# Strided-sparse attention and an ELU MLP on one core: load order, transposes, P v tiles and fillers of the first batches rearranged, and a half-step schedule for later scores and P v

## The chip, the core and the metric

The kernel runs on one core of one Trainium2 chip. The metric is the device time of one execution in microseconds (us). One core has five engines that matter here: TensorE (PE; matmuls, and PEld for its weight loads), VectorE (DVE), ScalarE (ACT), GpSimd (POOL) and the DMA queues. SBUF is the on-chip memory that holds the tiles; PSUM is the memory that TensorE's results go to, and this kernel uses eight banks of it.

The profile gives a "granted clock" of TensorE: 1.00 is full speed, 0.50 is half. "Fast" and "slow" mean here only that a run lies within, or above, 1.5% of the fastest run of the same kernel on that chip.

## The reference

```python
def _attn_ref(q, k, v):                       # 8 batches, 8 heads, 576 positions, 64 columns
    scores = scale * np.matmul(q, k.transpose(0, 1, 3, 2))
    rel = pos[:, None] - pos[None, :]
    mask_local   = (rel >= 0) & (rel < 32)                          # heads 0-3
    mask_strided = (rel >= 0) & (pos[None, :] % 32 == pos[:, None] % 32)   # heads 4-7
    ...                                       # masked softmax
    return np.matmul(attn, v)

def _moe_ref(x, w_in, w_out):                 # x: 4608 tokens x 512; w_in 512x2048; w_out 2048x512
    h = x @ w_in
    g = np.where(h > 0.0, h, np.exp(np.minimum(h, 0.0)) - 1.0)
    return g @ w_out
```

The output of the attention, heads side by side, is `x` of the MLP.

## The kernel before

The attention of one batch is cut in pieces: four pairs of heads (0 and 1 local, 2 and 3 strided), each with two halves `u`. The letters in the program's schedule strings are these.

- `T`: eight or six transposes each of q and k of a head pair on TensorE, through PSUM, and two copies to SBUF.
- `S`: scores of a half, exp on ACT, the mask multiplied in on DVE. The result is `pm`.
- `M`: row sums (`ones`) and P v of a half. `E`: logarithm and exp on ACT make the reciprocal of the sums, and DVE writes `xT`, the MLP's input. `X` is `M` and `E` together. `O` is the same work by another form, used from batch 3 on; there q and k are transposed by DMA.
- `f`: "fillers", matmuls on constants that only keep TensorE's clock up.
- `2`: one L2 group, four 128x512 matmuls of `g @ w_out`.
- `A` and `B`: `M` of batch 1's local heads in two-bank and in one-bank tiles. `t`: the strided transposes of batch 2. The small letters `c`, `m`, `v`, `a`, `w`, `x` are casts, masks and loads.

The MLP works on 256 tokens at a time: eight L1 groups (eight 128x256 matmuls of `x @ w_in`) and eight L2 groups. The first 16 L1 groups stand ahead of a loop of 128. I call its turns "steps". Attention of later batches is hung into the steps as jobs.

```python
    p_pm = ctx.enter_context(tc.tile_pool(name="pms", bufs=5))
    p_x = ...(name="ps_x", bufs=2, PSUM)      # two tiles of two banks ("wide")
    p_h = ...(name="ps_h", bufs=3, PSUM)      # three tiles of one bank
    p_o = ...(name="ps_o", bufs=1, PSUM)
    # --- loads of batch 0 (cut) ---
    load_vl(0, nc.gpsimd)
    load_str(0, qs, q)
    load_str(0, ks, k)
    ...
    load_str(0, vs, v)
    for i in range(2):
        nc.gpsimd.dma_start(out=w_in_sb[:, :, i * 1024:(i + 1) * 1024],
                            in_=w_in_v[:, :, i * 1024:(i + 1) * 1024])
    # --- batch 0 (cut) ---
    spins(24)
    ...
    for it in ("S0 c T1 S1 S2 S3 f4 M0 M1 E0 m T2 M2 E1 S4 E2 M3 T3 S5 E3 "
               "S6 M4 S7 E4 M5 E5 M6 E6 M7 f8 E7").split():
        ...
    # --- batch 1 among the L2 groups of the first 512 tokens (cut) ---
    for it in ("S4 2 S5 2 X4 2 S6 2 X5 2 S7 2 X6 2 X7 2 v "
               "a 2 T0 2 S0 T1 2 S1 S2 2 S3 w 2 A0 A1 2 B2 E0 E1 E2 A3 E3 x").split():
        ...
    # --- jobs of the loop (cut) ---
    SC = {2: (3, 6, 9, 12), 3: (18, 21.5, 25, 28.5)}
    SC.update({b: tuple(33 + 18 * (b - 4) + 4.5 * i for i in range(4)) for b in range(4, B)})
    at(4, lambda: casts(2))                   # six casts on GpSimd
    for b in (2, 3): ...                      # half u at step SC+u, its P v one step later
    for b in range(4, B):
        for i, p in enumerate((2, 3, 0, 1)):
            at(SC[b][i], lambda b=b, p=p: do(("SS", b, p)))       # both halves together
            at(SC[b][i] + 1.3, lambda b=b, p=p: do(("O", b, p, 0)))
            at(SC[b][i] + 2.5, lambda b=b, p=p: do(("O", b, p, 1)))
```

The softmax here doesn't subtract the row's maximum and nothing guards it: scores larger than these inputs give would overflow.

## Time and profile before

Three runs took 354.35 to 354.86 us, with a median of 354.75. The stages below are read from the starts of matmuls in TensorE's timeline of the profiled run, whose span is 352.3 us.

| point | us |
|---|---|
| first MLP matmul | 30.37 |
| first L2 group | 47.90 |
| step 0 of the loop | 73.63 |
| step 7 | 91.77 |
| step 16 (batch 3 begins) | 113.47 |
| step 33 (batches 4 to 7 begin) | 155.91 |
| end of the last matmul | 348.17 |

These are three lines of the profile's page: TensorE's busy time, the granted clock in 40 slices of 8.8 us (tenths, 9 is whole), and the shares of the chain of waits that ended last.

```profile
PE 320.1 (91%) x2896; PEld 223.6 (63%) x2896; DVE 247.6 (70%) x479; ACT 219.6 (62%) x426; POOL 111.2 (32%) x125
...
PEclk9556998989999999999999999989999999999999
...
PE 57%; DVE 17%; DMA 11%; ACT 8%; issue 3%; POOL 2%; DVEq 0%; SPq 0%; POOLq 0%; ACTq 0%
```

TensorE is busy 91% of the span, yet it makes up only 57% of the chain: in the first 155 us the chain goes through other engines and DMA. The clock is half in the second and third slice and in most of the fourth, and drops again in the seventh, the ninth and the 27th. From the clock's records, the half-clock stretches are 8.2 to 32.1, 52.6 to 56.0, 76.5 to 79.9 and 230.1 to 233.5 us.

The next view is the windows of kernel before. The columns are the window, its length, busy us and instruction counts of PE, PEld, DVE, ACT and POOL, the granted clock, the DMA share and GB/s. The windows are the opening, batch 1, and steps 0 to 7.

```profile
10.00:30.00 20.00, 15.99 (x183) 9.89 (x181) 10.40 (x25) 11.22 (x24) 5.48 (x8) 0.50 1.17 198
47.90:73.60 25.70, 21.31 (x208) 9.58 (x204) 12.61 (x25) 14.60 (x29) 6.33 (x8) 0.93 0.72 126
73.60:91.70 18.10, 14.26 (x162) 10.73 (x162) 12.60 (x22) 10.98 (x23) 10.65 (x10) 0.91 0.49 90
```

The opening has 4 us of gaps and half clock; the two other windows have about 4 us of gaps each. The gaps are named by TensorE's timeline of kernel before. Its columns are start, busy us, what ran, and in brackets the idle time ahead of it with what ended it.

```profile
17.45 0.66 PE L228 MATMUL tp<-identity,ks 72*128 72x72 bf16 x8 [1.01 <-DMA ks<-in_k_dram]
...
27.12 0.45 PE L328 MATMUL s_ps<-pm,ones 72*64 72x288 bf16 x2 [0.32 <-ACT ln L345]
...
28.07 0.45 PE L328 MATMUL s_ps<-pm,ones 72*64 72x288 bf16 x2 [0.26 <-ACT ln L345]
...
30.37 2.76 PE L388 MATMUL hpw<-xT,w_in_sb 128*128 128x256 bf16 x16
...
75.17 0.93 PE L362 MATMUL hps<-xT,w_in_sb 128*128 128x256 bf16 x7 [1.24 <-DVE xT L277]
...
84.36 0.31 PE L328 MATMUL so<-pm,ones 72*64 72x288 bf16 x2 [2.16 <-DVE pm L258]
```

The strided keys arrive at 17.45 us. At the end of the opening a P v piece comes every 0.95 us. At steps 0 to 7 TensorE waits 1.24 us for `xT` and 2.16 us for `pm`.

The last view of kernel before is the list of TensorE's waits in batch 3 (113 to 156 us): who waited for whom, us in total, times, and the longest.

```profile
PE ox L305 <- DVE pm L264: 2.8, 4, 0.8
PE sc L253 <- DMA ksT<-ks: 1.8, 2, 1.3
PE ox L305 <- DVE pm L258: 1.7, 3, 0.7
```

Nearly every P v piece of batch 3 waits for its mask product, because it stands only one step behind its scores.

### The profile page before, as it was taken

What the parts mean: (1) busy time and instruction counts of PE and PEld (TensorE: products, weight loads), DVE (VectorE), ACT (ScalarE), POOL (GpSimd) and SP (SyncE); (2) the same over time, 40 slices, a digit from 0 to 9 for tenths busy, and PEclk for the clock granted to TensorE, in tenths of its full rate; (3) what the DMA queues carried; (4) which work ended last, traced back from release to release, by engine and by line L of the source; (5) the groups of instructions that cost most, each with busy time, mean ns of one, the idle gap of its engine ahead of it and who ended that gap; (6) DMA issues with size and microseconds to landing.
All of it is one profiled execution on the core that took longest, in us unless ns stands there. A gap on an engine that the chain in (4) does not pass through costs nothing.

```text
span 352.3 us, 7511 instructions
## 1 busy us (share of the span) xinstructions
PE 320.1 (91%) x2896; PEld 223.6 (63%) x2896; DVE 247.6 (70%) x479; ACT 219.6 (62%) x426; POOL 111.2 (32%) x125
## 2 busy tenths in 40 slices
PE   6789979777989888889999999899999999999995
PEld 4447853355666565557767766667677777677762
DVE  2552982548777678868888889848988888666660
ACT  3545755565776676758776777567768787444441
POOL 8226610367256605333445451063500000000000
PEclk9556998989999999999999999989999999999999
DMA  8999993961598998099939971599356111111111
GB/s 181 181 205 204 210 169 52 186 129 21 113 174 176 140 187 196 11 154 183 197 94 146 225 178 32 104 163 233 92 100 106 32 36 54 34 31 30 41 50 60
DMA packets 49739, 43.24 MB, mean 123 GB/s; under 512 B 32809, under 2 KB 39721, under 8 KB 49705
## 3 DMA queue, kind: packets, MB, share of 16 engines
q0 software_dynamic: 15600, 25.77, 42.7%
q1 hardware_dynamic: 32624, 16.13, 22.1%
q10 hardware_dynamic: 1480, 0.88, 1.2%
q8 instruction: 22, 0.36, 0.5%
q14 instruction: 13, 0.10, 0.1%
HBM read 38.21 MB, written 9.44 MB: 135 GB/s over the span
## 4 chain that ended last, share of the span: by engine, by line
PE 57%; DVE 17%; DMA 11%; ACT 8%; issue 3%; POOL 2%; DVEq 0%; SPq 0%; POOLq 0%; ACTq 0%
PE ops L421 25%; PE hps L362 22%; DVE g L378 4%; DMA ksT<-ks 4%; DMA vl<-in_v_dram 4%; DMA ks<-in_k_dram 4%; DVE he L377 4%; PE ox L305 3%; PE sc L253 2%; DVE xT L277 2%; DVE xT L273 2%; ACT rc L311 2%; ACT ln L309 1%; ACT ln L308 1%; DVE g L398 1%
## 5 line engine op out<-in xcount | busy, mean ns | idle before, releaser
L421 PE MATMUL ops<-w_out_sb,g 128*128 128x512 bf16 x576 | 149.1, 384 | 0.0
L362 PE MATMUL hps<-xT,w_in_sb 128*128 128x256 bf16 x1088 | 144.1, 276 | 3.2 <-DVE xT L277 2.1
L362 PEld LDWEIGHTS <-w_in_sb 128*128 128x128 bf16 x1088 | 114.6, 114 | 19.0 <-issue 3.3
L370 ACT ACTIVATE he<-hps 128x512 f32<-128x512 f32 x136 | 80.5, 594 | 50.3 <-PE hps L362 49.8
L378 DVE TENSOR_TENSOR g<-he,hps 128x512 bf16<-128x512 bf16 x130 | 89.4, 688 | 13.9 <-DVE he L377 0.5
L421 PEld LDWEIGHTS <-g 128*128 128x128 bf16 x576 | 55.7, 99 | 38.7 <-issue 1.5
L377 DVE TENSOR_SCALAR he<-he 128x512 bf16<-128x512 f32 x130 | 62.2, 478 | 17.2 <-ACT he L370 15.6
L256 ACT ACTIVATE e<-sc 128x576 bf16<-128x576 f32 (+1 forms) x64 | 39.5, 646 | 22.8 <-PE sc L253 22.8
L426 ACT COPY osb<-ops 128x512 f32<-128x512 f32 x36 | 21.1, 587 | 11.4 <-PE ops L421 11.1
L308 ACT ACTIVATE ln<-ox 64x288 f32<-64x288 f32 x40 | 16.3, 408 | 17.2 <-PE ox L305 16.9
L273 DVE TENSOR_TENSOR xT<-ox,rc 64x288 bf16<-64x288 f32 x40 | 18.2, 454 | 11.0 <-ACT rc L311 10.6
L277 DVE TENSOR_TENSOR xT<-ox,rc 64x288 bf16<-64x288 f32 x40 | 18.2, 455 | 6.9 <-ACT rc L311 6.5
L264 DVE TENSOR_TENSOR pm<-e,mask_l 128x576 bf16<-128x576 bf16 x32 | 18.3, 590 | 6.1 <-ACT e L256 5.8
L111 POOL DMA_DIRECT2D qs<-in_q_dram x8 | 6.3, 788 | 47.4 <-DMA qsT<-qs 36.0
L258 DVE TENSOR_TENSOR pm<-e,mask_s 72x576 bf16<-72x576 bf16 x32 | 14.6, 473 | 8.4 <-ACT e L256 7.9
L132 POOL COPY vsx<-vs 72x1024 bf16<-72x1024 bf16 x10 | 11.5, 1174 | 28.3 <-DMA vs<-in_v_dram 21.1
L311 ACT ACTIVATE rc<-ln 128x288 f32<-128x288 f32 x40 | 17.7, 443 | 1.3
L117 POOL CAST qlb<-ql 72x1024 bf16<-72x1024 f32 x12 | 13.4, 1117 | 9.8 <-DMA ql<-in_q_dram 9.8
L309 ACT ACTIVATE ln<-ox 64x288 f32<-64x288 f32 x40 | 16.1, 402 | 0.5
L126 POOL CAST vlx<-vl 128x768 bf16<-128x768 f32 x15 | 13.2, 906 | 8.2 <-DMA vl<-in_v_dram 8.2
L122 POOL CAST klb<-kl 96x768 bf16<-96x768 f32 x13 | 11.6, 891 | 9.9 <-DMA kl<-in_k_dram 9.9
L111 POOL DMA_DIRECT2D vs<-in_v_dram x8 | 5.7, 715 | 26.3 <-PE so L338 21.7
(87 smaller groups left out, 268.3 us busy)
## 6 DMA issues: line engine op xcount, KB each, us to landing
vl<-in_v_dram POOLq DMA_DIRECT2D x8, 576.0 KB, 16.9
out_dram<-osb SPq DMA_DIRECT2D x32, 144.0 KB
kl<-in_k_dram POOLq DMA_DIRECT2D x7, 576.0 KB, 14.1
ql<-in_q_dram POOLq DMA_DIRECT2D x7, 576.0 KB, 15.0
qs<-in_q_dram POOLq DMA_DIRECT2D x8, 288.0 KB, 6.7
ks<-in_k_dram POOLq DMA_DIRECT2D x8, 288.0 KB, 9.5
vs<-in_v_dram POOLq DMA_DIRECT2D x8, 288.0 KB, 10.7
w_in_sb<-in_moe_w_in_dram POOLq DMA_DIRECT2D x2, 1024.0 KB, 19.0
```

The costliest lines, as they stand in the source:

```text
L256: nc.scalar.activation(e[0:R], sc[0:R, :, 0:W], ACT.Exp, scale=scale)
L273: nc.vector.tensor_mul(xs[:, u * W:(u + 1) * W], o[pr], rc[pr])
L277: nc.vector.tensor_mul(dst, o[pr].rearrange(pat, b=3, s=NS), rc[pr].rearrange(pat, b=3, s=NS))
L308: nc.scalar.activation(ln[lo], o[0][hi], ACT.Ln)
L309: nc.scalar.activation(ln[hi], o[1][lo], ACT.Ln)
L311: nc.scalar.activation(rc, ln, ACT.Exp, scale=-1.0)
L362: nc.tensor.matmul(hps[:, mm], lhsT=w_in_sb[:, c, (m // 4) * 512:(m // 4 + 1) * 512].rearrange("c (p mm) -> c mm p", mm=4)[:, m % 4], rhs= ...
L370: nc.scalar.activation(e, hps, ACT.Exp)
L377: eng.tensor_scalar(e1, e, scalar1=1.0, scalar2=1.0, op0=ALU.min, op1=ALU.subtract)
L378: nc.vector.tensor_tensor(gt, e1, hps, op=ALU.max)
L421: nc.tensor.matmul(ops, lhsT=g[:, m, kk * 128:(kk + 1) * 128], rhs=w_out_sb[:, m, :], start=(m == 0), stop=(m == MC - 1))
L426: nc.scalar.copy(o_sb, ops)
```

## The change

The change wants fewer waits in the first 155 us. It has these parts.

1. Batch 0: the strided q, k and v are loaded ahead of the local v. Transposes go through tiles of one bank. All scores run first, then all P v. Fillers stand between the pieces.
2. Batch 1: P v of the local heads in one-bank tiles; two more L2 groups and the strided transposes of batch 2 (`t`) move into this stage from the loop.
3. Batch 2: its casts run at step 2 instead of 4, and batch 3's local data are loaded right behind them. Batch 3's strided q and k are loaded before the loop (`x`).
4. All of batches 2 to 7: a half-step grid. The scores of half `u` run at SC + 0.5u and their P v at SC + 1.5 + 0.5u, each half by itself. Five `pm` buffers become eight.

Smaller parts are left out here: among others, which engine casts v of batch 0, on which queue one load of q stands, and the order of the L2 groups of the second 256 tokens.

The core of the diff, with cuts marked:

```diff
-    p_pm = ctx.enter_context(tc.tile_pool(name="pms", bufs=5))
+    p_pm = ctx.enter_context(tc.tile_pool(name="pms", bufs=8))
...
-    load_vl(0, nc.gpsimd)
     load_str(0, qs, q)
     load_str(0, ks, k)
...
+    load_str(0, vs, v)
     nc.gpsimd.iota(dist, ...)
-    load_str(0, vs, v)
+    load_vl(0, nc.gpsimd)
...
+    def piece_T(b, hp, engs=None, wide=True):
+        if wide:
+            pw = p_x.tile([128, 2, 1024], BF16, tag="x", name="tp2")
+            ps = [pw[:, 0, 0:S], pw[:, 1, 0:S]]
+        else:
+            ps = [p_h.tile([128, S], BF16, tag="h", name="tp") for _ in range(2)]
...
-    for it in ("S0 c T1 S1 S2 S3 f4 M0 M1 E0 m T2 M2 E1 S4 E2 M3 T3 S5 E3 "
-               "S6 M4 S7 E4 M5 E5 M6 E6 M7 f8 E7").split():
+    for it in ("f4 S0 S1 c f4 T1 m S2 f4 T2 S3 f4 S4 T3 f4 S5 f4 S6 M4 f2 S7 f2 E4 M5 f2 E5 M6 f2 E6 "
+               "v M7 f2 E7 M0 f2 E0 M1 f2 E1 M2 f2 E2 M3 f8 E3").split():
...
-    for it in ("S4 2 S5 2 X4 2 S6 2 X5 2 S7 2 X6 2 X7 2 v "
-               "a 2 T0 2 S0 T1 2 S1 S2 2 S3 w 2 A0 A1 2 B2 E0 E1 E2 A3 E3 x").split():
+    for it in ("2 S4 2 S5 2 2 X4 2 S6 X5 2 S7 2 X6 2 X7 v "
+               "a 2 2 T0 2 S0 S1 2 T1 B0 2 S2 B1 E0 2 S3 E1 B2 2 B3 E2 2 t E3 x").split():
...
-    SC = {2: (3, 6, 9, 12), 3: (18, 21.5, 25, 28.5)}
+    SC = {2: (2, 5, 9.5, 12.5), 3: (16.5, 20.5, 24.5, 28.5)}
...
-    at(4, lambda: casts(2))
+    at(2, casts2)          # cast_k, cast_q of batch 2, load_kl/ql(3), cast_v, load_vl(3)
...
-    for b in range(4, B):
-        for i, p in enumerate((2, 3, 0, 1)):
-            at(SC[b][i], lambda b=b, p=p: do(("SS", b, p)))
-            at(SC[b][i] + 1.3, lambda b=b, p=p: do(("O", b, p, 0)))
-            at(SC[b][i] + 2.5, lambda b=b, p=p: do(("O", b, p, 1)))
+    for b in range(2, B):
+        for i, p in enumerate((2, 3, 0, 1)):
+            for u in range(2):
+                at(SC[b][i] + .5 * u, lambda b=b, p=p, u=u: do(("S", b, p, u)))
+                at(SC[b][i] + 1.5 + .5 * u,
+                   lambda b=b, p=p, u=u: do(("X" if b == 2 else "O", b, p, u)))
```

## The prediction

> **What bounds the kernel now.** TensorE: busy 320.1 of 352.3 us (engine table).  In the undisturbed stretch after 155 us, eight 128x256 matmuls and four 128x512 matmuls each take 0.86 us (timeline); 144 groups of each make 248 us, and attention of batches 1 to 7, from the same timeline (0.27 us a score piece, 0.26 to 0.42 a P v piece, 0.53 a transposed pair), about 37 us. That is 285 us. With an opening of 30.4 us (first MLP matmul in the timeline) and 4 us of last store, about 33 us are waits and half-clock time. Waits rule the first 155 us.
>
> **Where the time is (TensorE timeline, stage windows).**
> - Opening, 0 to 30.4 us. Clock 0.50 from 10 to 30 us. Strided transposes wait until 17.45 us for ks; P v then runs at 0.95 us a piece.
> - First MLP part, 30.4 to 47.7: 17.3 us for 14.8 us of work; the first 3 us run at half clock.
> - Batch 1, 47.7 to 73.4: 5.6 us of idle gaps. Clock 0.83 in two windows (50-60, 70-80): matmul groups of 0.86 take 1.7 us after the gaps.
> - Batches 2 and 3, 73.4 to 155: gaps of 2.16 (pm), 0.88, and 0.5 to 0.75 before most batch-3 P v pieces (pm), 1.34 for ksT.
>
> The Trainium skill, "TensorE: Matmul & The Clock Gate", Part 1, says that the clock is halved by an idle activity window of about 3.4 us and restored by a busy one. The trace agrees: both drops follow 1.4 to 1.6 us of gaps and last about one such window.
>
> **What the change does.**
> 1. Opening: ks and vs stand ahead of v in the queue. Estimated from about 200 GB/s: ks at 11-12 us instead of 17.4. One-bank transpose tiles let ACT copy klT without following DVE (0.45 us). All eight score pieces run first, then P v without interruption: 19 us + 8 x 0.9 + 1.7 = about 28 us to the first MLP matmul, if the 48 fillers (0.11 us each, 5 us; were 12 and 8 small ones) keep the clock. At half clock they would cost 10 us and the opening would take 32. I expect mostly full clock: -2.5 us, and -1.5 in the MLP part after it.
> 2. Batch 1: local P v in one-bank tiles, no longer competing with scores for the two wide buffers; batch 2's strided transposes cover the last xT. Gaps 5.6 to about 2.5, one or both half-clock windows gone: -4 us. Two L2 groups (1.7 us) move here from the loop.
> 3. Batch 2: transposes out of the loop, no half-clock window at 76 us, but six MLP steps without L2, where DVE (1.1 us a step plus attention) binds: -2.
> 4. Batch 3, and the half-step schedule (P v 1.5 steps after scores): most 0.5-0.75 gaps go, ksT arrives earlier: -4.
> 5. Batches 4 to 7: pm gaps of about 1.3 us go; ksT waits (1.34, 1.98 with 1.7 of half clock) stay: -0.5.
>
> Sum -14.5, partly shared, so -13.5: **341 us, range 333 to 349**. Chances: faster by over 2% 0.86, within 2% 0.12, slower 0.02.
>
> **What would show it.** First MLP matmul near 28 us; ks transposes before 13.5 us; granted clock above 0.75 in 10 to 30 us; TensorE gaps in batches 2 and 3 together under 4 us.
>
> **What would make it wrong.** Fillers at half clock delaying the chain (clock 0.5, opening 32 us); ks not earlier because the queues share bandwidth; DVE binding in the L2-free steps; more half-clock windows, or ksT waits growing in batches 4 to 7.

## The result and the profile after

Three runs took 349.60 to 350.58 us, with a median of 350.46. The ratio to kernel before is 0.9875 (95% interval 0.9848 to 0.9902). Every ratio here is the mean time of one kernel's fast runs over the mean of the other's fast runs of the same rounds, so it is not quite the ratio of the medians quoted. The gain is 1.2%: 4.3 us of the 13.5 predicted. The time lies above the upper end of the range, and the change falls under "within 2%", to which I had given 0.12.

The stages of the two profiled runs, with the changes that I predicted for them:

| stage | before | after | change | predicted |
|---|---|---|---|---|
| opening, to the first MLP matmul | 30.37 | 30.08 | -0.29 | -2.5 |
| to the first L2 group | 17.53 | 17.08 | -0.45 | -1.5 |
| batch 1, to step 0 | 25.73 | 26.09 | +0.36 | -4 |
| steps 0 to 7 | 18.14 | 18.40 | +0.26 | -2 |
| steps 7 to 16, rest of batch 2 | 21.70 | 21.89 | +0.19 | in the -2 |
| steps 16 to 33, batch 3 | 42.44 | 36.29 | -6.15 | -4 |
| step 33 to the last matmul | 192.26 | 194.96 | +2.70 | -0.5 |

Only batch 3 gained what was hoped for. The same three lines of the page, of kernel after:

```profile
PE 323.0 (93%) x2926; PEld 222.9 (64%) x2926; DVE 247.1 (71%) x479; ACT 221.0 (63%) x426; POOL 109.2 (31%) x125
...
PEclk9658999996999999999999999999999999999999
...
PE 68%; ACT 12%; DVE 11%; DMA 4%; issue 3%; SPq 1%; ACTq 0%; DVEq 0%
```

DMA has left the chain, from 11% to 4%, and TensorE's share rose. But the clock still drops in the opening, and again near 80 us, there longer than before. The half-clock stretches are now 11.8 to 28.9 and 80.1 to 86.9 us; the late one at 230 us is gone. The same windows of kernel after:

```profile
10.00:30.00 20.00, 18.44 (x194) 10.93 (x195) 9.03 (x23) 11.81 (x24) 8.73 (x10) 0.57 1.13 194
47.20:73.30 26.10, 22.75 (x255) 11.42 (x253) 13.65 (x27) 15.64 (x31) 7.31 (x9) 1.00 0.95 174
73.30:91.60 18.30, 12.40 (x136) 9.08 (x133) 12.99 (x22) 10.37 (x23) 11.15 (x13) 0.81 0.82 159
```

The opening: TensorE is busier by 2.5 us in the same 20 us, at nearly the same clock, and nothing came of it. Busy time is not progress where it is fillers. Batch 1: full clock, and more work in the same time. Steps 0 to 7: less TensorE work than before (12.40 against 14.26 us busy), in the same time, at a lower clock. TensorE's timeline of kernel after shows the places:

```profile
10.89 0.43 PE L233 MATMUL tp<-identity,klb 96*128 96x96 bf16 x6 [1.61 <-ACT klb L120]
...
13.55 0.67 PE L233 MATMUL tp<-identity,ks 72*128 72x72 bf16 x8
...
24.13 0.45 PE L333 MATMUL s_ps<-pm,ones 72*64 72x288 bf16 x2
24.37 0.45 PE L343 MATMUL o_ps<-pm,vs 72*64 72x72 bf16 x8
24.75 0.61 PE L436 MATMUL idle<-warm 128*128 128x256 bf16 x2
25.29 0.45 PE L339 MATMUL s_ps<-pm,ones 128*64 128x288 bf16 x2
...
30.08 0.27 PE L393 MATMUL hpw<-xT,w_in_sb 128*128 128x256 bf16 x1
...
74.90 1.80 PE L367 MATMUL hps<-xT,w_in_sb 128*128 128x256 bf16 x15 [1.38 <-DVE xT L282]
...
81.75 0.45 PE L333 MATMUL so<-pm,ones 72*64 72x288 bf16 x2 [3.69 <-DVE pm L263]
```

The ks transposes do come at 13.55 us, 3.9 earlier and without a wait. But a gap of 1.61 us stands ahead of them, and the clock falls at 11.8 us. At the half clock a P v piece takes 1.16 us (24.13 to 25.29) with no gap at all, and 0.54 of it (24.75 to 25.29) are two fillers at half clock. Before it took 0.95. In steps 0 to 7 the wait for `pm` grew from 2.16 to 3.69 us.

What made `pm` late is in the timeline of VectorE of kernel after (same columns):

```profile
76.98 2.23 DVE L379 SCALAR_TENSOR_TENSOR g<-he,he 128x512 bf16<-128x512 f32 x1 [2.13 <-ACT he L378]
79.13 1.04 DVE L382 TENSOR_SCALAR he<-he 128x512 bf16<-128x512 f32 x1
80.28 0.69 DVE L383 TENSOR_TENSOR g<-he,hps 128x512 bf16<-128x512 bf16 x1
80.88 1.81 DVE L263 TENSOR_TENSOR pm<-e,mask_s 72x576 bf16<-72x576 bf16 x2
```

And of GpSimd of kernel after, in the same time:

```profile
76.85 0.83 POOL L120 CAST klb<-kl 96x768 bf16<-96x768 f32 x1
77.62 1.03 POOL L117 CAST qlb<-ql 72x1024 bf16<-72x1024 f32 x1
...
80.54 1.84 POOL L126 CAST vlx<-vl 128x768 bf16<-128x768 f32 x2
```

The first instruction takes 2.23 us where it takes 0.69 elsewhere. It lies beside two casts on GpSimd. The `pm` products (1.81 for two, 0.82 undisturbed) lie beside two others. The merge at 80.28, which has one operand in PSUM, takes its usual 0.69.

The casts are not new in this stage. GpSimd works 10.65 us in it before and 11.15 after, by the windows above, and in before too VectorE is stretched beside the casts. From VectorE's timeline of kernel before:

```profile
77.25 1.51 DVE L374 SCALAR_TENSOR_TENSOR g<-he,he 128x512 bf16<-128x512 f32 x1 [2.13 <-ACT he L373]
```

And from GpSimd's timeline of kernel before:

```profile
76.41 0.83 POOL L122 CAST klb<-kl 96x768 bf16<-96x768 f32 x1
77.18 1.04 POOL L117 CAST qlb<-ql 72x1024 bf16<-72x1024 f32 x1
```

Summed over the stage, the instructions of these three kinds (the first, the second and the `pm` products) take 2.3 us more than undisturbed (0.69, 0.425 and 0.45 us) in before and 3.1 more in after.

Last, TensorE's waits in batch 3 of kernel after, in answer to the three lines of before:

```profile
PE ops L426 <- ACT osb L431: 0.9, 4, 0.2
```

The waits for `pm` and for `ksT` are gone.

### The profile page after: what moved, and what is told of

It is laid out like the page before. It is cut to its first block, busy times and chain, and to the rows that moved or that the text cites. A ratio compares the mean times of both kernels' runs of the same rounds, so it can differ in the third digit from the quotient of the medians.

```text
span 348.9 us, 7582 instructions
## 1 busy us (share of the span) xinstructions
PE 323.0 (93%) x2926; PEld 222.9 (64%) x2926; DVE 247.1 (71%) x479; ACT 221.0 (63%) x426; POOL 109.2 (31%) x125
## 4 chain that ended last, share of the span: by engine, by line
PE 68%; ACT 12%; DVE 11%; DMA 4%; issue 3%; SPq 1%; ACTq 0%; DVEq 0%
PE ops L426 28%; PE hps L367 27%; PE sc L258 4%; DVE he L382 3%; ACT he L375 3%; DVE g L383 2%; DMA kl<-in_k_dram 2%; ACT osb L431 2%; PE idle L436 2%; DMA ksT<-ks 2%; PE ox L310 1%; ACT ln L314 1%; ACT ln L313 1%; PE tp L233 1%; PE hpw L393 1%
## 5 line engine op out<-in xcount | busy, mean ns | idle before, releaser
L426 PE MATMUL ops<-w_out_sb,g 128*128 128x512 bf16 x576 | 146.9, 380 | 3.6 <-ACT osb L431 3.6
L367 PEld LDWEIGHTS <-w_in_sb 128*128 128x128 bf16 x1088 | 116.1, 114 | 22.4 <-issue 2.8
L383 DVE TENSOR_TENSOR g<-he,hps 128x512 bf16<-128x512 bf16 x130 | 89.4, 688 | 14.3 <-PE hps L367 1.0
L382 DVE TENSOR_SCALAR he<-he 128x512 bf16<-128x512 f32 x130 | 63.4, 488 | 25.2 <-ACT he L375 24.2
L426 PEld LDWEIGHTS <-g 128*128 128x128 bf16 x576 | 52.0, 98 | 44.5 <-issue 5.3
L261 ACT ACTIVATE e<-sc 128x576 bf16<-128x576 f32 (+1 forms) x64 | 41.0, 647 | 18.7 <-PE sc L258 18.6
L269 DVE TENSOR_TENSOR pm<-e,mask_l 128x576 bf16<-128x576 bf16 x32 | 15.5, 496 | 6.7 <-ACT e L261 6.5
L263 DVE TENSOR_TENSOR pm<-e,mask_s 72x576 bf16<-72x576 bf16 x32 | 15.9, 513 | 4.9 <-ACT e L261 4.9
L132 POOL COPY vsx<-vs 72x1024 bf16<-72x1024 bf16 x10 | 10.7, 1095 | 25.0 <-DMA vs<-in_v_dram 25.0
L436 PE MATMUL idle<-warm 128*128 128x256 bf16 x74 | 16.1, 367 | 1.3 <-DVE warm L155 1.3
```

The lines of the kernel that those rows point to most:

```text
L261: nc.scalar.activation(e[0:R], sc[0:R, :, 0:W], ACT.Exp, scale=scale)
L367: nc.tensor.matmul(hps[:, mm], lhsT=w_in_sb[:, c, (m // 4) * 512:(m // 4 + 1) * 512].rearrange("c (p mm) -> c mm p", mm=4)[:, m % 4], rhs= ...
L382: eng.tensor_scalar(e1, e, scalar1=1.0, scalar2=1.0, op0=ALU.min, op1=ALU.subtract)
L383: nc.vector.tensor_tensor(gt, e1, hps, op=ALU.max)
L426: nc.tensor.matmul(ops, lhsT=g[:, m, kk * 128:(kk + 1) * 128], rhs=w_out_sb[:, m, :], start=(m == 0), stop=(m == MC - 1))
L436: nc.tensor.matmul(ps, lhsT=warm[:, 0:128], rhs=warm[:, 0:ps.shape[-1]], start=True, stop=True, skip_group_check=True)
```

## The experiments

I had three questions, with a theory and a rival for each. The runs were made in four sessions on four chips. The medians of kernel before there were 354.71, 354.57, 355.06 and 355.04 us, over 7 to 11 runs each. In the third session only two of the eleven runs of kernel before count as fast, because one of them took 348.32 us; the ratios of that session are weak, and there the medians say more.

A stage scatters even where its code is the same. In eight profiled runs with the opening of kernel after, the first MLP matmul lies at 28.39 to 32.64 us and the first L2 group at 45.22 to 48.78. In the ten in which steps 0 to 7 and what stands just ahead of them are those of kernel after, these steps take 17.55 to 18.40 us. In all sixteen with batch 3 as changed, steps 16 to 33 take 36.2 to 37.8. In the twelve with the half-step grid to the end, step 33 to the last matmul takes 192.92 to 194.96, and the first trace of kernel after is the longest of these. Where I give a difference of two single traces below, read it against these ranges.

- The opening. Theory: at half clock the fillers are themselves the chain. Rival: the loads (w_in above all) bound the opening, whatever the fillers do.
- Steps 0 to 7. Theory: GpSimd's casts slow VectorE through the memory that both read. Rival: without L2 groups among these steps VectorE simply has too much work, and the casts change nothing.
- Batches 4 to 7. Theory: the half-step grid costs what the batch-3 gain brought. Rival: the difference is the draw of the clock.

### Opening: the fillers taken out (first session)

```diff
-    for it in ("f4 S0 S1 c f4 T1 m S2 f4 ... E1 M2 f2 E2 M3 f8 E3").split():
+    for it in ("S0 S1 c T1 m S2 T2 S3 S4 T3 S5 S6 M4 S7 E4 M5 E5 M6 E6 "
+               "v M7 E7 M0 E0 M1 E1 M2 E2 M3 f8 E3").split():
```

> The changed kernel without the 24 + 16 small fillers of the opening (the 26 at the start and the 8 before the MLP stay). Theory A (with the clock at half, the fillers are themselves the chain: in the changed kernel TensorE is 99% busy from 20 to 30 us and a P v piece takes 1.16 us, of which 0.54 us are two fillers): the clock stays at 0.5 all the same, but a P v piece falls back to about 0.95 us, the first MLP matmul comes at 27.5 to 28.5 us instead of 30.1, and the kernel gains 1 to 2.5 us (348 to 349.5). Theory B (the opening is bound by the order of loads and the ACT and DVE chain, fillers only fill): first MLP matmul unchanged at 30 us, time 350.5 or slower, since the clock comes back later.

Measured: 350.05 us (349.00 to 352.01, 4 runs), ratio 0.9901 (0.9837 to 0.9965). The first MLP matmul is at 27.84 instead of 30.08, ahead of all eight openings with fillers, and at half clock all the same. So the fillers were the chain at half clock, as the theory has it. But the second weight load then waits for w_in, and the clock stays half until 33.0, as TensorE's timeline of this run shows:

```profile
29.38 3.39 PE L393 MATMUL hpw<-xT,w_in_sb 128*128 128x256 bf16 x15 [1.12 <-DMA w_in_sb<-in_moe_w_in_dram]
```

These 15 matmuls take 3.39 us instead of 1.8. The first L2 group comes at 47.47, against 47.16 with fillers, and so inside the range of the eight. The rival is right about what stands behind the fillers: both bounds lie close together.

### Opening: fillers where the gap was (first session)

```diff
+            if i and mid:
+                spins(mid)              # between the two halves of one transposed pair
...
-            piece_T(0, n, None, False)
+            piece_T(0, n, None, False, 14 if n == 1 else 0)
```

> The changed kernel with 14 more fillers between the two halves of batch 0's second local transposes, where TensorE sat idle for 1.61 us just before the clock was halved. Theory A: that gap is what cost the clock; with it filled the half-clock stretch begins at 15 us or later instead of 11.8, and the first MLP matmul comes 1 to 2 us earlier (349). Theory C: the clock falls anyway at the next window, because the small pieces do not count as enough activity, and nothing is gained (350 to 351).

Measured: 349.49 us (346.90 to 351.88, 4 runs), ratio 0.9877 (0.9794 to 0.9960). In the profiled run the clock holds until 80.3 us, and the mean clocks of the four runs are 0.984 to 0.995. From TensorE's timeline:

```profile
27.12 0.27 PE L395 MATMUL hpw<-xT,w_in_sb 128*128 128x256 bf16 x1
...
29.19 1.83 PE L395 MATMUL hpw<-xT,w_in_sb 128*128 128x256 bf16 x15 [1.79 <-DMA w_in_sb<-in_moe_w_in_dram]
```

The opening is 3 us shorter, 1.79 of which go to the wait for w_in. The first L2 group is at 45.65, 1.5 earlier than in the first trace of after, but inside the range of the eight openings. The fillers leave 1.02 us of the gap, and the clock was kept in this execution; behind it w_in binds. That the gap costs the clock is seen over all traces here: without these fillers the clock of after's opening, or of one close to it, falls between 11.0 and 14.0 us in ten traces of ten; with them it is whole through the opening in four of six, and falls at 14.3 and 21.2 us in the others.

### Opening: w_in in four loads of one tile (second session)

```diff
-    for i in range(2): dma_start(out=w_in_sb[:, :, i * 1024:(i + 1) * 1024], ...)
+    for i in range(4): dma_start(out=w_in_sb[:, :, i * 512:(i + 1) * 512], ...)
```

This stands on top of the filled gap.

> The kernel of the gap-filling run, with w_in loaded in four quarters of 512 columns in place of two halves. Theory H (with the clock restored the opening is bound by the landing of w_in's first half at 29.2 us, which TensorE awaited for 1.79 us there): the first quarter lands about 2.5 us sooner, the wait shrinks to under 0.5 us, and the second batch of MLP work is 1.3 to 1.8 us earlier than in the gap-filling run (its first L2 matmul at 44 us instead of 45.65). Rival I (the queue's order, not the size of its pieces, sets the landing): the wait stays above 1.2 us.

Measured: 348.53 us (347.87 to 350.92, 4 runs), ratio 0.9872 (0.9801 to 0.9943). From TensorE's timeline:

```profile
29.12 1.83 PE L395 MATMUL hpw<-xT,w_in_sb 128*128 128x256 bf16 x15 [1.28 <-DMA w_in_sb<-in_moe_w_in_dram]
```

That is a miss: the wait ends at the same time. The semaphores of the trace say why. The first weight load waits for that of the first quarter, which landed at 20.90 us. The second, which needs the same quarter, waits for that of the fourth, which landed at 29.07. The dependency of this program is on the tile, not on the part that is read, so smaller loads into one tile released nothing earlier.

### Opening: w_in in four tiles (third and fourth session)

```diff
-    w_in_sb = const([128, KC, d_ff], BF16, "w_in_sb")
+    w_in_q = [const([128, KC, 512], BF16, f"w_in_q{i}") for i in range(4)]
...
-                    lhsT=w_in_sb[:, c, (m // 4) * 512:(m // 4 + 1) * 512].rearrange(
+                    lhsT=w_in_q[m // 4][:, c].rearrange(
```

Also on top of the filled gap.

> The gap-filling kernel with w_in in four tiles of their own. In the run with four quarters of one tile nothing came sooner, and the program shows why: the second weight load of the first MLP group waits for the landing of all four quarters, not of its own. Theory H2 (so the landing of the whole of w_in at 29.1 us bounds the opening): with own tiles TensorE passes the first MLP group without a wait above 0.3 us, at about 27.4 us, and the first L2 matmul comes at 43.5 to 44.2 us (45.4 with one tile), unless the next quarters are then awaited. Rival: the first quarter alone lands at 29 us too, and the wait of 1.3 us stays.

Measured: 347.53 us (345.18 to 350.87, 4 runs), ratio 0.9899 (0.9739 to 1.0059). The profiled run was the slowest of the four, and the one that counts as slow; the ratio leaves it out. It lost the clock at 14.3 us and kept it half until 31.3, so its first MLP matmul came at 31.39. Nothing about w_in could be read from it.

> The gap-filling kernel with four w_in tiles once more, for a profile in which the clock is held. In the runs with one tile the whole of w_in landed at 29.1 us and was awaited there by the second weight load; the first of two halves landed near 24 us. With the clock held I expect the first MLP group at 27.2 to 27.7 us in one piece, without a wait, and the first L2 matmul at 43.5 to 44.2 us (45.4 with one tile). If the clock is lost again this says nothing.

Measured: one run of 348.69 us, clock 0.989, with the clock whole through the opening. From TensorE's timeline:

```profile
26.37 0.27 PE L394 MATMUL hpw<-xT,w_in_q 128*128 128x256 bf16 x1
...
26.86 1.80 PE L394 MATMUL hpw<-xT,w_in_q 128*128 128x256 bf16 x15 [0.22 <-DVE xT L283]
```

The wait for w_in is gone, and the first L2 group is at 43.44, against 45.38 in one tile. So some 2 us of the opening, one trace against one with the clock whole in both, were a dependency wider than the data. The two profiles together also say that even the filled gap does not hold the clock in every execution.

### Opening: the old load order (fourth session)

```diff
+    load_vl(0, nc.gpsimd)
     load_str(0, qs, q)
     load_str(0, ks, k)
...
-    load_vl(0, nc.gpsimd)
```

> The changed kernel with v of batch 0 loaded first, as before the change. If the load order is worth what I predicted (strided k at 11 to 12 us instead of 17.4), the strided transposes wait to 16 or 17 us, the whole queue of strided pieces moves back by 3 us, and the first MLP matmul comes at 32 to 33.5 us instead of 30.1: 2 to 3 us slower than the changed kernel. If the opening is bound by the fillers at half clock from 17 us on, and has slack before, under 1 us is lost.

Measured: 351.98 us (350.67 to 353.59, 4 runs), ratio 1.000 (0.9914 to 1.0085). The clock was half from 12.0 to 32.5. From TensorE's timeline:

```profile
16.08 0.66 PE L233 MATMUL tp<-identity,qs 72*128 72x72 bf16 x8 [3.94 <-DMA qs<-in_q_dram]
...
17.66 0.66 PE L233 MATMUL tp<-identity,ks 72*128 72x72 bf16 x8 [0.92 <-DMA ks<-in_k_dram]
```

The first MLP matmul is at 33.98, 3.9 us later than in the first trace of kernel after. Most of that can be the clock: in another trace with the opening of after and nearly the same half-clock stretch (12.2 to 32.6; it is that of the run with two L2 groups back in the loop, below) the first MLP matmul is at 32.64. At equal clock the new load order is thus worth 1.3 us here, in the new order of pieces, which asks for the strided data first. In the total, 1.5 us remain by the medians, inside the scatter.

### Steps 0 to 7: no casts of batch 2 (first session)

The six casts on GpSimd are left out and the loads kept. The result is wrong (relative error 0.197).

```diff
     def casts2():
-        for a in range(2):
-            cast_k(nc.gpsimd, a)
-            cast_q(nc.gpsimd, a)
         load_kl(3, nc.gpsimd)
         load_ql(3, nc.gpsimd)
-        for a in range(2):
-            cast_v(nc.gpsimd, 2, a)
         load_vl(3, nc.gpsimd)
```

> Wrong result on purpose: the changed kernel without the six casts of batch 2 on POOL, its loads kept. Theory D (POOL's casts hold up those VectorE instructions that have all operands in SBUF: 2.23 us for one of 0.69, 1.04 for one of 0.42, 1.81 for two of 0.82, and these make the 3.69 us gap and the half-clock stretch at 80 us): the durations of VectorE between 75 and 85 us are back at 0.69, 0.42 and 0.45 us, the gap shrinks to under 1.5 us, the half-clock stretch there is gone, and loop step 7 begins 3 to 5 us earlier (346 to 348). Theory E (VectorE has simply too much work in steps without L2): the gap stays above 2.5 us, gain under 1 us.

Measured: 344.26 us (343.97 to 348.07, 4 runs), ratio 0.9756 (0.9679 to 0.9833). Steps 0 to 7 take 14.55 us, 3.85 less than after. VectorE's timeline shows three of the instructions listed for kernel after:

```profile
75.74 0.69 DVE L379 SCALAR_TENSOR_TENSOR g<-he,he 128x512 bf16<-128x512 f32 x1 [2.13 <-ACT he L378]
...
77.34 0.69 DVE L383 TENSOR_TENSOR g<-he,hps 128x512 bf16<-128x512 bf16 x1
77.95 0.82 DVE L263 TENSOR_TENSOR pm<-e,mask_s 72x576 bf16<-72x576 bf16 x2
```

TensorE's wait for `pm`, from its timeline:

```profile
78.45 0.31 PE L333 MATMUL so<-pm,ones 72*64 72x288 bf16 x2 [1.63 <-DVE pm L263]
```

The first instruction is back at 0.69, `pm` at 0.82, and the wait fell from 3.69 to 1.63. There is no half-clock stretch after 21.4 us in this trace. The rival falls: the same VectorE work, without the casts beside it, is 3.85 us faster, and still 3.0 faster than the shortest of the ten traces with the casts. The gap gives 2.06 of the 3.85; the other 1.8 fits the half-clock stretch of 6.8 us that is missing: in the second trace of kernel after this stretch is 3.4 us long, and the stage is 0.7 shorter.

### Steps 0 to 7: the casts moved (second session)

Two casts go to ACT at step 0, and the other four stay on GpSimd, behind step 7.

```diff
     def casts2():
-        for a in range(2):
-            cast_k(nc.gpsimd, a)
-            cast_q(nc.gpsimd, a)
+        cast_k(nc.gpsimd, 1)
+        cast_q(nc.gpsimd, 1)
...
-    at(2, casts2)
+    at(0, lambda: (cast_k(nc.scalar, 0), cast_q(nc.scalar, 0)))
...
-    at(SC[2][1] + 2, lambda: load_str(3, vs, v))
+    at(SC[2][1] + 2, lambda: load_str(3, vs, v), casts2)
```

> Correct result: the changed kernel with batch 2's first two casts on ACT at loop step 0 (where ACT sat idle 2 us) and the other four on POOL only after loop step 7. If theory D is right (POOL's casts next to VectorE in the steps without L2 cost 3.9 us), steps 0 to 7 take 15 to 16 us instead of 18.4 and the half-clock stretch at 80 us goes; some of it comes back after step 7, where the four casts now run. In all 2 to 3.5 us faster than the changed kernel (347 to 348.5). If the delay of batch 3's loads (14 us later) matters, it shows as waits of TensorE in batch 3 (steps 16 to 33) and the gain is lost.

Measured: 346.49 us (344.91 to 349.11, 4 runs), ratio 0.9809 (0.9731 to 0.9888), correct. Steps 0 to 7 take 14.08 us, 4.3 less than after; 0.6 comes back in steps 7 to 13 (16.00 against 15.38). Until the casts begin at 87.64 us, VectorE's instructions take their undisturbed times. It is the same gain with a right result, so it was the place of the casts, not the amount of work.

### Steps 0 to 7: the last xT earlier (second session)

```diff
-               "a 2 2 T0 2 S0 S1 2 T1 B0 2 S2 B1 E0 2 S3 E1 B2 2 B3 E2 2 t E3 x").split():
+               "a 2 2 T0 2 S0 S1 2 T1 B0 2 S2 B1 E0 2 S3 E1 B2 2 B3 E2 E3 2 t x").split():
```

> The changed kernel with the last softmax tail of batch 1 before its last L2 group and batch 2's transposes, in place of behind them. Theory J (the tail's Ln waits on ACT behind the copy of an L2 result, its last product on VectorE behind four transpose copies; both together make the 1.38 us gap before loop step 0's second matmul): the gap goes, steps 0 and 1 are 1.2 to 1.5 us earlier. Whether it reaches the end depends on theory D: VectorE is the bound in steps 2 to 6, so I expect 0.5 to 1.4 us (349 to 350).

Measured: 348.40 us (346.26 to 350.52, 4 runs), ratio 0.9851 (0.9756 to 0.9947). The gap of 1.38 us for `xT` at step 0 is gone, but the next one, for `pm`, grew to 5.22, and steps 0 to 7 take 17.77, no less than the ten traces' 17.55 to 18.40. Under the casts VectorE binds, so a wait taken away ahead of it comes back behind it.

### Steps 0 to 7: two L2 groups back in the loop (third session)

```diff
-               "a 2 2 T0 2 S0 S1 ... B3 E2 2 t E3 x").split():
+               "a 2 T0 2 S0 S1 ... B3 E2 t E3 x").split():
```

> The changed kernel with two L2 groups back in the loop (14 instead of 16 done before it). Theory D (POOL's casts slow VectorE in steps 0 to 6, with TensorE left waiting): the loop starts 1.7 us earlier, the 3.69 us gap at step 2 stays, as no L2 stands in front of it, and the L2 groups at steps 5 and 6 take up part of the later waits: 0 to 0.8 us faster. Theory K (steps without L2 are the loss in themselves): steps 0 to 7 no longer than in the changed kernel although they hold two more groups, 1.5 us faster in all.

Measured: 351.14 us (349.57 to 352.68, 4 runs). The ratio is 1.0024 (0.9889 to 1.0160). By the medians it is 351.14 against 349.78 for an unchanged kernel after in the same session. Steps 0 to 7 take 18.62 us, with 1.73 us more work in them. The groups fit into the waits, but where they were taken away nothing was gained: batch 1 and steps 0 to 7 together take 43.86 us, against 44.49 and 43.81 in the two traces of kernel after. Where the L2 groups stand is worth nothing that shows here.

### Batches 4 to 7: the old schedule (first session), and half of it (second session)

First the whole old schedule for batches 4 to 7, with the rest as changed; then only the scores of both halves together, with P v in its new place.

```diff
-    for b in range(2, B):
+    for b in (2, 3):
...
+    for b in range(4, B):
+        for i, p in enumerate((2, 3, 0, 1)):
+            at(int(SC[b][i]) + .5, lambda b=b, p=p: do(("SS", b, p)))
+            at(int(SC[b][i] + 1.3) + .5, lambda b=b, p=p: do(("O", b, p, 0)))
+            at(int(SC[b][i] + 2.5) + .5, lambda b=b, p=p: do(("O", b, p, 1)))
```

> The changed kernel with the old schedule for batches 4 to 7 (both score pieces of a head pair together, P v 1 and 2 to 3 steps later), all else as changed. Theory F (two separate score pieces and the wait for the L2 bank behind the ACT queue cost about 0.2 and 0.22 us per head pair, and make the 2.7 us that the changed kernel gives back after batch 3): 2 to 3 us faster than the changed kernel (347.5 to 348.5), no waits of L2 matmuls for the osb copy in batches 4 to 7. Theory G (the half-step schedule is what removed the ksT waits and the half-clock stretch at 230 us): these come back and the time is 351 or more.

```diff
+            if b > 3:
+                at(SC[b][i], lambda b=b, p=p: do(("SS", b, p)))
             for u in range(2):
-                at(SC[b][i] + .5 * u, lambda b=b, p=p, u=u: do(("S", b, p, u)))
+                if b <= 3:
+                    at(SC[b][i] + .5 * u, lambda b=b, p=p, u=u: do(("S", b, p, u)))
```

> The changed kernel with both score pieces of a head pair together in batches 4 to 7, and P v at the new half steps. The old schedule there made steps 33 to the end 5.7 us shorter. If the split of the scores is the larger part (each separate piece costs about 0.1 us more than half a pair, 4 pairs and 4 batches: 1.5 to 3 us), this run gains 2 to 3 us over the changed kernel and the L2 waits for the osb copy stay (2.7 us). If the position of P v is the larger part, it gains under 1.5 us.

Measured: the old schedule 345.83 us (344.08 to 347.22, 4 runs), ratio 0.9762 (0.9683 to 0.9841); the half 346.95 us (345.80 to 348.36, 4 runs), ratio 0.9817 (0.9748 to 0.9886). From step 33 to the last matmul: 194.96 (after), 192.22 (scores together), 189.25 (all old), 192.26 (before). No clock is lost after 100 us in the profiled runs of the three changed kernels (before has 3.4 us of half clock there), so these lengths are free of it, and the rival, the draw of the clock, falls. By these single traces splitting the scores costs 2.7 us and the new places of P v cost 3.0. But they scatter (192.92 to 194.96 with the grid in twelve traces, 189.21 to 190.68 with the old schedule in three), so the grid costs 2.2 to 5.8 us, and the shares are rough. Steps 51 to 60 are free of the scatter and show both: 18.53 or 18.54 us in all twelve, 18.09 with scores together, 17.66 in all three with the old schedule. So the first part costs 0.44 us there and the second 0.43, over two head pairs. For the second, the waits of TensorE from 150 to 345 us. Kernel after:

```profile
PE ops L426 <- ACT osb L431: 2.7, 6, 0.8
PE ox L310 <- DVE pm L269: 1.5, 1, 1.5
```

The old schedule:

```profile
PE ox L310 <- DVE pm L269: 1.3, 2, 0.8
PE hps L367 <- DVE xT L282: 0.5, 1, 0.5
PE ox L310 <- DVE pm L263: 0.5, 1, 0.5
```

The 2.7 us for `osb` are L2 matmuls that wait until ACT has copied the last result out of the one PSUM bank of `p_o`. In the kernel with scores together they are still there (2.7 us, 6 times); in the old schedule they are gone. In steps 51 to 60 such a wait stands once (0.29 us idle), and lengthens an L1 group from 0.87 to 1.33 us, start to start. The cost of the split is no wait. The starts in TensorE's timeline show it in the same steps: two score pieces take 0.24 us each and the L1 group between them 1.00, where both together take 0.37 and the L1 group behind them 0.90. That is 0.22 us per head pair, by estimate 3.5 us for 16 pairs if all are alike.

### The changed kernel again (third session)

Kernel after unchanged, to see its scatter.

> The changed kernel once more, beside the runs to follow on the same chip. No theory expects another mean than before: ratio 0.985 to 0.99, with single runs spread by some 4 us as those of the kernel before are here, since each execution draws another set of half-clock stretches (mean clock 0.96 to 0.98).

Measured: 349.78 us (348.01 to 351.27, 6 runs). The ratio is 0.9987 (0.9897 to 1.0078), against the two fast runs of kernel before; by the medians it is 349.78 over 355.06, or 0.985. In this trace the opening is 1.5 us shorter and steps 0 to 7 are 0.7 shorter than in the first trace, from the same program. Over the eight traces with this opening the first MLP matmul lies within 4.3 us and the first L2 group within 3.6, so smaller differences of two traces in the opening prove nothing here unless the clock's stretches are alike.

### All repairs together (third session), and with more fillers (fourth session)

The first kernel has the filled gap, four w_in tiles, the moved casts, the earlier `xT`, and the old schedule for batches 4 to 7.

> All that helped, together: gap filled in the opening, w_in in four tiles, batch 2's casts split between ACT and a later time on POOL, the last tail of batch 1 ahead of its L2 group, and the old schedule in batches 4 to 7. If the parts are independent, as the traces say (opening 1.5 to 3 us, steps 0 to 7 about 4 us, tail 1 us, batches 4 to 7 5.7 us), it is 11 to 14 us faster than the changed kernel: 336 to 340 us, ratio 0.950 to 0.960. If they hand time to one another (DMA waits in batches 3 to 4 because the loads of batch 3 come later and the stretch before them is shorter), 340 to 343.

Measured: 340.91 us (339.49 to 344.16, 6 runs), ratio 0.9744 (0.9627 to 0.9861), or 0.960 by the medians. The profiled run lost the clock from 21.2 to 28.0, in the P v part, where two fillers stand in each piece. The second kernel has three or four there:

```diff
-               ... S6 M4 f2 S7 f2 E4 M5 f2 E5 M6 f2 E6 v M7 f2 E7 M0 f2 E0 M1 f2 E1 M2 f2 E2 ...
+               ... S6 M4 f3 S7 f3 E4 M5 f4 E5 M6 f4 E6 v M7 f4 E7 M0 f4 E0 M1 f4 E1 M2 f4 E2 ...
```

> The combination with three or four fillers in place of two between the P v pieces of batch 0. At full clock a P v piece then takes about 0.95 to 1.1 us on TensorE instead of 0.8 to 0.95, at half clock 1.6 instead of 1.16 us. If the fillers hold the clock there, the first MLP matmul comes at 27.5 to 28.5 us in the profile, no half-clock stretch between 14 and 28 us, and the time is within 1 us of the combination (340 to 341); if the clock is lost all the same, the first MLP matmul comes at 31 us or later and it is 2 us slower.

Measured: 337.92 us (336.81 to 340.58, 6 runs), ratio 0.9608 (0.9534 to 0.9683), correct. The mean clocks of the six runs are 0.997 to 1.000; those of the first kernel's six were 0.968 to 1.000. The windows of this kernel, for the opening and for steps 0 to 7:

```profile
10.00:30.00 20.00, 17.96 (x245) 13.01 (x243) 9.71 (x24) 12.70 (x26) 9.80 (x12) 1.00 1.21 195
...
69.70:82.50 12.80, 10.26 (x139) 8.28 (x136) 9.65 (x22) 11.29 (x23) 2.00 (x3) 1.00 0.44 77
```

GpSimd works 2.00 us in steps 0 to 7, against 11.15 in kernel after, and the stage takes 12.8 us instead of 18.4. The lengths of the stages against the first trace of kernel after: opening 26.52 (3.6 less), steps 0 to 7 12.78 (5.6 less), steps 7 to 33 59.65 (1.5 more), step 33 to the end 189.21 (5.7 less); the rest is equal within 0.4. This version beats both kernels: 3.9% below before by the fast runs of its session (4.8% by the medians), and 3.4% below the 349.78 of kernel after, which is of another session. That four fillers hold the clock where two don't is six runs against six, with the clock's own draw in them; it is likely, not settled.

## Why the prediction was wrong

The predicted time, 341 us, and its range from 333 to 349 missed 350.46 us; the direction was right, and the size of the gain was not. By its steps:

**Step 1, opening, -2.5 and -1.5: failed.** The load order did what was said: ks at 13.55 us instead of 17.45, worth 1.3 us at equal clock by the run with the old load order (3.9 against the first trace of after). The failing step is "I expect mostly full clock". I had named its failure as the first risk ("clock 0.5, opening 32 us"), and it came so, with the clock at 0.57 from 10 to 30 us and an opening of 30.08. The page "TensorE: Matmul & The Clock Gate" of the Trainium skill, Part 1, gives the rule that I used, an idle window throttles and a busy one restores. The trace does not agree: no window was idle. A gap of 1.61 us, with one of 0.55 in the same window, was enough to lose the clock, and it stayed lost for 17 us in which TensorE was 99% busy by its records. How long is a draw: in the second trace of the same program it was 6.8 us, and the opening 1.5 shorter. What I had not considered at all is w_in: 1.8 us behind the fillers, by the run with the filled gap.

**Step 2, batch 1, -4: right in kind, half in size.** The clock is 1.00 instead of 0.93. The stage takes 0.36 us longer, but it has taken in two L2 groups (1.73 us) and two transposed pairs (1.06 us at 0.53 each), so the same work runs 2.4 us faster. Two waits of 0.80 us for the logarithm on ACT remain; I take it from the program, and no run shows it, that this is because three one-bank tiles hold only one and a half P v pieces.

**Step 3, batch 2, -2: failed.** The 2.8 us that moved out should have shortened steps 0 to 7 to about 15.35; they take 18.40. "DVE (1.1 us a step plus attention) binds" was right as far as it went, but its cost was wrong: VectorE's instructions stretch while GpSimd casts, and so TensorE's work taken out of the stage left a wait behind (3.69 us for `pm`, before 2.16). The Trainium skill, "SBUF — State Buffer", section "Who interferes with whom", says that VectorE instructions with two SBUF inputs, or in the two-port modes, share a port pair with GpSimd, and that the one that comes second is blocked. The trace agrees. Over the whole trace of after, TENSOR_SCALAR `he` takes 0.425 us in the mean with nothing on GpSimd beside it (94 times) and 0.653 with something (36 times), at most 2.01. The merge with one operand in PSUM takes 0.688 either way. The run without casts shows the cost in the stage, 3.85 us, and the run with the casts moved gets 4.3 back. Against before this is only part of the account. There the same six casts lie in the same stage, and stretch VectorE by 2.3 us instead of 3.1. So the casts show why the stage does not get shorter, and not that the change brought them; that it would have kept its 18.14 us in before without the moves is not tested.

**Step 4, batch 3, -4: right, undersized.** It measured -6.15 us in the pair of traces, and -4.6 to -6.2 over the sixteen traces. The waits for `pm` (4.5 us in before) and for `ksT` (1.8) are gone from the list, which is 6.3 together; my term had counted only "most" of them. No run puts batch 3 alone back, so the shares of the half-step grid, the earlier loads and the three more `pm` buffers are not shown.

**Step 5, batches 4 to 7, -0.5: failed.** It measured +2.70, and +0.7 at the least over the twelve traces with this grid. The waits for `ksT` that I expected to stay are gone from the list (3.3 us in before), and so is the half clock at 230 us. But the half-step grid costs some 3 us by splitting the scores and some 3 by the places of P v, 2.2 to 5.8 in all by the traces. With the old schedule there the same stage takes 189.21 to 190.68 us, 1.6 to 3.1 less than in before (whose half clock at 230 us is part of that). I saw the regrouping in the diff and gave it no cost.

**Where the expected gain went.** In us, by the two traces and against the stages predicted: 3.3 were not gained in the opening and the first MLP part; 6.6 from the first L2 group to step 7; 3.2 in batches 4 to 7; batch 3 gave 2.2 more than predicted, and 0.2 went in steps 7 to 16. That is 11.1 short of the unshared sum of 14.5, which leaves the 3.4 us by which the profiled runs differ.

## What to carry to other kernels

A filler is free only where something else is the chain and the clock is whole; at half clock it costs twice and may be the chain itself, so place fillers in the one gap that loses the clock and check the next bound behind it (here a load whose tile was wider than what the first matmul needs). Before moving work to GpSimd, look at what VectorE runs at that time: all-SBUF instructions there took 1.5 to 1.6 times as long in the mean and up to three to five times (2.23 us for 0.69, 2.01 for 0.425), while those with a PSUM operand did not notice (0.69 either way). A stage that another engine paces does not get shorter when TensorE's work is taken out of it. When one schedule suits the stage that starves (batch 3), do not give it to the stages that were already full (batches 4 to 7) without measuring them by themselves. And one trace of a stage is not yet a measurement: the same opening took 28.39 to 32.64 us in eight.

## What the Trainium skill lacked or had wrong

- "TensorE: Matmul & The Clock Gate", Part 1, "What's actually happening", gives the idle condition as at least one idle window of about 3.4 us. The window's length agrees: all half-clock stretches here that end before the last matmul are multiples of about 3.4 us (3.4, 6.8, 10.2, 17.1, 20.5, 23.9). But no idle window is needed: the clock of kernel after fell at 11.8 us behind a window with gaps of 1.61 and 0.55 us, and that of before at 52.6 us behind one with gaps of 1.44 and 0.19. Cut into these windows of 3.41 us, the seventeen traces hold 30 drops: ahead of 29 the window has, by the records, 1.48 to 3.39 us without a matmul, ahead of one 0.60 (at 21.2 us, among P v pieces); and no window at full clock that kept it has more than 1.75. Where a gap falls decides too: gaps of 1.33 and 0.55 us in one window lost the clock in the first run of four tiles, gaps of 1.42 and 0.55 in two windows kept it in the run with four loads of one tile. The page's section "A second HAM failure mode: psum-queue depth-cycling" mentions short idles between matmul groups, without a figure for how short.
- The same page gives a busy window as enough to restore the clock. In kernel after TensorE was 99% busy by its records from 11.8 to 28.9 us and the clock stayed half, over five such windows. What ran in the last nine us were small P v pieces (72 or 128 rows by 64 columns, moving at most 288 columns) and two fillers a piece; with three or four fillers a piece the clock was 0.997 or more in six of six runs. The page does not say which matmuls count as activity, except for transposes (Part 4), and no run here separates the kinds.
- The same page, under the same heading, puts the penalty of the ramp at a kernel's start at under 1% of a typical kernel and calls it variable from run to run. It gives no spread for clock that is lost later: the runs of the kernel with the filled gap lie between 346.90 and 351.88 us (1.4%), at mean clocks of 0.984 to 0.995.
- "SBUF — State Buffer", "Who interferes with whom", is right about who is slowed but its only sizes are two single measurements (6.8 times for VectorE, 1.5 for GpSimd), none for a kernel in which both engines run all the time: here TENSOR_SCALAR went from a mean of 0.425 to 0.653 us (36 times), the local `pm` product from 0.454 to 0.721 (5 times only), and one SCALAR_TENSOR_TENSOR from 0.69 to 2.23.
- The same section gives no figure for VectorE beside GpSimd's issue of DMAs alone. In the run without casts one TENSOR_SCALAR still took 0.89 us beside one. Over the seventeen traces TENSOR_SCALAR `he` took 0.409 to 0.431 us with nothing on GpSimd beside it (1610 times), and up to 1.155, with a mean of 0.51, beside DMA issues alone (230 times). The `pm` products stayed at 0.445 to 0.459 beside such issues (100 times).
